# Last unit of a convolution and gated feed-forward kernel: 768 of 1024 tokens projected with Wo standing, the last 256 by tokens

## Chip, cores and metric

The kernel runs on one core of one Trainium2 chip. The metric is the device time in microseconds (us) of one execution, the median of several. All five engines of the core work in it: TensorE (PE, with its weight loads PEld), VectorE (DVE), ScalarE (ACT), GpSimd (POOL) and SyncE (SP, which issues DMAs here).

## What is computed

Two layers follow each other. A causal convolution over 7 positions along the sequence has one softmax-normalised filter for each of 8 heads (24 channels each). Its output, seen as 32768 tokens of 192 channels, goes through a gated feed-forward layer of width 1536. Inputs and output are float32.

```python
def _attn_ref(x, weight):                       # x: 8 x 4096 x 192, weight: 8 x 7
    w = softmax(weight)
    x_pad = concat([zeros(B, 6, D), x], axis=1)
    x_unf = x_pad[:, idx, :].reshape(B, S, K, H, group)
    return einsum('hk,bskhg->bshg', w, x_unf).reshape(B, S, D)

def _moe_ref(x, w_gate, w_val, w_out):          # 192 x 1536, 192 x 1536, 1536 x 192
    gate = maximum(x @ w_gate, 0.0)
    val = x @ w_val
    return gate * val @ w_out
```

## The kernel before, in words

**Tiling.** The eight sequences are taken as two streams (`st` 0 and 1) of four sequences, which are worked on side by side. A window is `WIN` = 512 tokens of each stream, a unit is two windows (`UNIT` = 1024 tokens of each stream), and there are `NUNIT` = 16 units, 0 to 15. All matmuls take 16-bit operands and add up in PSUM in float32. The kernel's order is written out by hand: on each engine the instructions run in the order of the source, and the waits between engines are put in by the framework from what each instruction reads and writes.

**A unit.** `gate_val` (L576 on, matmul at L596) makes the gate and the value of one window in 12 slices `f` of 128 hidden channels. For each slice ScalarE applies the relu to the gate (L607) and VectorE multiplies it by the value out of PSUM into `hT`, 16 bits (L608). `hT` holds hidden channels on its partitions and tokens along them. After both windows the unit is projected by Wo.

**The projection of units 0 to 14** (`project_turn`, L618) holds Wo still and streams tokens. Wo's 192 output channels are cut into three groups `p` of 64 columns, which are two sets of 32 channels. A matmul takes 64 hidden channels by 64 output channels and streams 512 tokens, so that four of them fill the array. The result has output channels on its partitions; VectorE turns it in blocks of 32 by 32 (`turn_out`, L636) into the output tile `o`. `store` (L645) sends `o` to memory with eight DMAs on SP's queue, of 32 partitions each. Rows there are 96 channels, 384 bytes. While this goes on the engines also make the convolution of a later unit (`product`, `lane_rest`, `add`); the last unit has no such work.

**The projection of unit 15** (`project`, L661) goes the other way round: 128 tokens of `hT` are the weights, and Wo's 192 columns stream. It needs no turn, since tokens come out on the partitions. It is called four times, for window 0 and 1 and both streams, 4 x 12 matmuls each. In the fourth call the 512 tokens are cut into pieces of 256, 128 and 128, each with a PSUM tile `ps` of its own. Copies (L672) are ScalarE's but for the second last, which is VectorE's. The stores (L675) go from SP's queue, the very last from ScalarE's.

**Pools.** PSUM has four buffers of `[128, 2, 512]` float32, that is two banks each, handed out in turn. The output pool has two buffers, so the tile `o` of a unit takes the place of that of two units before, and waits until that one's stores are done.

Of the kernel before, what the change touches and what calls it, by code (L numbers as in the profile page):

```python
# [8 lines left out]
FP = mybir.dt.float32  # L9
# [6 lines left out]
def kernel(  # L16
# [12 lines left out]
    nc = tc.nc  # L29

    B, S, D = x.shape
# [4 lines left out]
    NB = B // 2  # L36
    NCH = D // 64
    NBLK = D // 32
    NFF = DFF // 128
    WIN = 512  # L40
# [10 lines left out]
    UNIT = 2 * WIN  # L51
    NUNIT = NB * S // UNIT
# [17 lines left out]
    opool = ctx.enter_context(tc.tile_pool(name="opool", bufs=2))  # L70
    psum = ctx.enter_context(tc.tile_pool(name="psum", bufs=4, space=bass.MemoryType.PSUM))
# [92 lines left out]
    with nc.allow_low_precision("one of the terms is not zero"):  # L164
        nc.vector.tensor_reduce(
            out=Z[:, 112 : 112 + HR],
            in_=eye[:].rearrange("p (g i) -> p i g", i=HR),
# [4 lines left out]
        out=mask[:, :, 0],  # L172
        in_=eye[:].rearrange("p (g i) -> p g i", i=HR),
# [6 lines left out]
    Wo = const.tile([128, NFF, 3, 64], F16)  # L180
# [4 lines left out]
    def none(reps, n):  # L185
        z = zeros[:, 0:1]
        return bass.AP(tensor=z.tensor, offset=z.offset, ap=[z.ap[0], [0, reps], [1, n]])
# [23 lines left out]
    for part, heads in zip(raised, BANDS):  # L211
        nc.tensor.matmul(
            out=part[:, 0 : SUB * len(heads)],
            lhsT=zeros[:],
            rhs=none(len(heads), SUB),
            start=True,
            stop=False,
            skip_group_check=True,
# [65 lines left out]
    for s in (8, 9):  # L284
# [5 lines left out]
        out=mx[:], in_=spread[:, 0, 0:KW], axis=mybir.AxisListType.X, op=ALU.max, negate=True  # L290
# [5 lines left out]
    for jj in STEPS0[:3]:  # L296
# [5 lines left out]
        out=prod[:],  # L302
# [8 lines left out]
    for heads in BANDS:  # L311
        n = len(heads)
        nc.vector.scalar_tensor_tensor(
            out=blocks[:, heads[0] : heads[0] + n, :],
# [12 lines left out]
    for part, heads, to, copy in zip(  # L327
        raised, BANDS, bands, [nc.vector.tensor_copy] * 3
    ):
        n = len(heads)  # L330
        for j in range(128 // HR):
# [3 lines left out]
                out=part[:, 0 : SUB * n].rearrange("p (h t) -> p h t", t=SUB)[:, :, s0 + lo : s0 + hi],  # L335
                lhsT=Z[:, 112 - HR * j : 240 - HR * j],
                rhs=blocks[:, heads[0] : heads[0] + n, lo:hi],
                start=False,
                stop=(j == 128 // HR - 1),
                skip_group_check=True,  # L340
# [5 lines left out]
    for c in range(NCH):  # L346
        r0 = 0
        while r0 < 64:
            h = (64 * c + r0) // G
            r1 = min(64, G * (h + 1) - 64 * c)  # L350
            row = wn[HR * h : HR * h + 8, :]
            for st in range(2):
                nc.sync.dma_start(
                    out=tap[64 * st + r0 : 64 * st + r1, c, :],
                    in_=bass.AP(
                        tensor=row.tensor,
                        offset=row.offset,
                        ap=[row.ap[0], [0, (r1 - r0) // 8], [1, KW]],
                    ),
# [95 lines left out]
    def lane_halo(b):  # L455
        xr = rpool.tile([128, NCH, 2 * (HALO + WIN)], F16, name="x_r")
        if b:
            end = second_start(b - 1) + WIN
            nc.gpsimd.tensor_copy(out=xr[:, :, 0:HALO], in_=xrs[b - 1][:, :, end - HALO : end])
        at = second_start(b)  # L460
        if at > HALO + WIN:
            nc.gpsimd.memset(xr[:, :, at - HALO : at], 0.0)
        xrs[b] = xr

    def lane_turn(b):
        xe, head = xes.pop(b)
        if b not in xrs:
            lane_halo(b)
        xr, at = xrs[b], second_start(b)
        n = 4 * len(windows(b))  # L470
        xp = epool.tile([128, TILES, NCH, 2, 64], F16, name="x_p")
        parts = [slice(0, n)] if head is None else [slice(0, n // 2), slice(n // 2, n)]
        for st in range(2):
            for js in parts:
                nc.gpsimd.tensor_copy(out=xp[:, js, :, st, :], in_=xe[:, js, st, :, :])  # L475
        for j in range(n):
            to = HALO + 128 * j if j < 4 else at + 128 * (j - 4)
            nc.sync.dma_start_transpose(
                out=xr[:, :, to : to + 128],
                in_=xp[:, j].rearrange("p c s r -> p (c s r)"),  # L480
            )
        if head is not None:
            turned = const.tile([HALO, NCH, 2, 64], F16, name="turned")
            for st in range(2):
                nc.gpsimd.tensor_copy(out=turned[:, :, st, :], in_=head[:, st, :, :])
            nc.sync.dma_start_transpose(
                out=xr[:, :, 0:HALO], in_=turned[:].rearrange("p c s r -> p (c s r)")
            )
# [141 lines left out]
    def between_turns(ps):  # L630
        nc.scalar.copy(out=turned_by[:], in_=ps[:, :, 0])  # L631
# [6 lines left out]
            in_=ps[:].rearrange("p b (t c) -> p b t c", c=32),  # L638
        )

    def store(o, bp, w0):
        for q in range(4):
            row0 = (bp + NB * (q // 2)) * S + WIN * w0
            for b in range(2):
                nc.sync.dma_start(  # L645
                    out=out[
                        row0 + WIN * b : row0 + WIN * (b + 1), D // 2 * (q % 2) : D // 2 * (q % 2 + 1)
                    ].rearrange("(t p) d -> p t d", p=32),
                    in_=o[32 * q : 32 * q + 32, :, D // 2 * b : D // 2 * (b + 1)],
                )  # L650

    def project(bp, w, h, st, stores, final, o):


        parts = [range(4)] if not final else [range(2), range(2, 3), range(3, 4)]
        row0 = (bp + NB * st) * S + WIN * w
        for n, qs in enumerate(parts):
            ps = psum.tile([128, 2, 512], FP, name="ps")
            for i, q in enumerate(qs):
                for f in range(NFF):  # L660
                    nc.tensor.matmul(  # L661
                        out=ps[:, i // 2, D * (i % 2) : D * (i % 2) + D],
                        lhsT=h[:, f, st, 128 * q : 128 * (q + 1)],
                        rhs=Wo[:, f, :, :].rearrange("k p (a d) -> k a p d", a=2),
                        start=(f == 0),
                        stop=(f == NFF - 1),
                    )
            os_ = o[:, qs[0] : qs[0] + len(qs), :].rearrange("p (a b) d -> p a (b d)", a=(len(qs) + 1) // 2)
            k = len(qs)
            a, m = (k + 1) // 2, min(k, 2) * D  # L670
            copy = nc.vector.tensor_copy if n == 1 else nc.scalar.copy
            copy(out=os_, in_=ps[:, 0:a, 0:m])  # L672
            nq = max(1, k // stores)
            for q0 in range(qs[0], qs[0] + k, nq):
                (nc.scalar if n == 2 else nc.sync).dma_start(  # L675
                    out=out[row0 + 128 * q0 : row0 + 128 * (q0 + nq), :].rearrange(
                        "(q p) d -> p q d", p=128
                    ),
                    in_=o[:, q0 : q0 + nq, :],
                )  # L680


    dense[0] = xcpool.tile([128, 2, NCH, WIN], F16, name="xc")
# [5 lines left out]
    for c, copy in enumerate((nc.scalar.copy, nc.vector.tensor_copy, nc.scalar.copy)):  # L689
# [7 lines left out]
        out=plain.rearrange("p (c d) -> p c d", d=D), in_=moe_w_out.rearrange("(c p) d -> p c d", p=128)  # L697
    )
    for u in range(NUNIT):
        if u == 0:  # L700
            lane_turn(0)
            wide = plain.rearrange("k (f a p d) -> k f a p d", a=2, p=3, d=32)
            for a in range(2):
                nc.gpsimd.tensor_copy(out=Wo[:, :, :, 32 * a : 32 * a + 32], in_=wide[:, :, a, :, :])
            lane_halo(1)
            lane_load(1)
        hs = [gate_val(u, w) for w in range(2)]
        if u == 0:
            dense[1] = xcpool.tile([128, 2, NCH, WIN], F16, name="xc")
        bp, w0 = u * UNIT // S, u * UNIT % S // WIN  # L710
        lane = None
        if u < NBLOCK:
            lane_first(u)
            lane = lane_rest(u)
        if u == 0:
            conv(2)
        o = opool.tile([128, UNIT // 64, D], FP, name="out_s")
        if u == NUNIT - 1:
            for i in range(4):
                project(bp, w0 + i // 2, hs[i // 2], i % 2, (4, 2, 1, 1)[i], i == 3, o[:, 4 * i : 4 * i + 4, :])  # L720
            continue
        tiles = [None] * 3
        for p, turn in ((0, 0), (1, 0), (0, 1), (2, 0), (1, 1), (2, 1)):
            if turn == 0:
                tiles[p] = psum.tile([128, 2, 512], FP, name="ps")
            project_turn(hs, p, tiles[p], turn)
            if turn == 0:
                between_turns(tiles[p])
                if lane:
                    for k in TAPS[p]:  # L730
                        product(u, k)
                continue
            if lane:
                for _ in range(STEPS[p]):
                    next(lane)
            turn_out(tiles[p], o, p)
        store(o, bp, w0)
        if lane:
            add(u, 0)
        if u + 1 < NBLOCK:  # L740
            lane_turn(u + 1)
        if len(windows(u)) > 1:
            add(u, 1)
        if u + 2 < NBLOCK:
            lane_load(u + 2)
# [30 lines left out]
```

## Time and profile before

Three runs took 761.95 us in the median (761.77 to 762.75). The profiled execution took 761.94 us, with a span of 760.2 us from its first to its last instruction and a granted TensorE clock of 0.999.

| engine | busy us | share of the span | instructions |
|---|---|---|---|
| PE (matmuls) | 756.1 | 99% | 13724 |
| PEld (weight loads) | 471.5 | 62% | 13724 |
| DVE | 675.8 | 89% | 647 |
| ACT | 611.1 | 80% | 681 |
| POOL | 455.3 | 60% | 299 |

How to read it: an engine is busy while one of its instructions runs, and matmuls overlap, so that the mean duration of a matmul (376 ns for 512 columns) is longer than the time by which one follows the other. The chain of waits is followed back from the last instruction, at each step to what released it or to the instruction before it on its engine; 65% of the span is in the gate and value matmuls (L596), 31% in the projection of units 0 to 14 (L618) and 2% in that of unit 15 (L661). Times in the timeline count from the start of the span. SPq and ACTq are the queues from which SP and ScalarE issue DMAs.

### The profile page before, as it was taken

Reading aid. Unit: us, or ns where it says so; the run is one execution under the profiler, and the core shown is the slowest. Engines: PE = TensorE matmul, PEld = TensorE weight load, DVE = VectorE, ACT = ScalarE, POOL = GpSimd, SP = SyncE. Lnnn points to the kernel's source line nnn. Section 1 sums busy time; section 2 is a strip of 40 time slices with the busy share of each in tenths; the row PEclk is TensorE's granted clock in tenths of the full one; section 3 lists DMA queues with packets and bytes.
Section 4 is the critical chain, followed back from the end, with each engine's and each line's share of the span. In section 5 each row is a group of like instructions: output and inputs, shape, how many; then the busy total and the mean of one; then the engine's idle time right before and its main releaser. Section 6 shows DMA issues by size and latency. Waiting matters only on the chain.

```text
span 760.2 us, 30519 instructions
## 1 busy us (share of the span) xinstructions
PE 756.1 (99%) x13724; PEld 471.5 (62%) x13724; DVE 675.8 (89%) x647; ACT 611.1 (80%) x681; POOL 455.3 (60%) x299
## 2 busy tenths in 40 slices
PE   9999999999999999999999999999999999999998
PEld 5555556666666666666666666666666666666668
DVE  7889989998998989989999899998999989897891
ACT  7897887878878788887877878788797887877671
POOL 8519649195591946829377392874919659193600
PEclk9999999999999999999999999999999999999999
DMA  9954532345424444334444334453244532240402
GB/s 149 136 72 92 79 79 52 43 96 75 85 44 51 98 66 85 54 58 83 64 85 73 56 76 54 85 85 64 60 49 93 77 78 52 23 101 7 85 2 85
DMA packets 154146, 54.23 MB, mean 71 GB/s; under 512 B 149264, under 2 KB 154016, under 8 KB 154016
## 3 DMA queue, kind: packets, MB, share of 16 engines
q1 hardware_dynamic: 117488, 37.83, 24.5%
q0 software_dynamic: 36096, 14.16, 16.5%
q8 instruction: 107, 1.75, 0.9%
q10 hardware_dynamic: 432, 0.30, 0.1%
q14 instruction: 23, 0.19, 0.1%
HBM read 29.21 MB, written 25.17 MB: 72 GB/s over the span
## 4 chain that ended last, share of the span: by engine, by line
PE 99%; DMA 1%; ACT 0%; SPq 0%; issue 0%
PE ps L596 65%; PE ps L618 31%; PE ps L661 2%; DMA prod<-in_x_dram 1%; PE ps L390 0%; PE ps L413 0%; ACT out_s L122 0%; SPq L112 0%; ACT out_s L672 0%
## 5 line engine op out<-in xcount | busy, mean ns | idle before, releaser
L608 DVE TENSOR_TENSOR hT<-gr,ps 128x1024 f16<-128x1024 f16 (+1 forms) x385 | 468.9, 1218 | 35.4 <-ACT gr L607 8.3
L607 ACT ACTIVATE gr<-ps 128x1024 f16<-128x1024 f32 (+1 forms) x385 | 393.2, 1022 | 114.2 <-PE ps L596 114.2
L525 POOL TENSOR_TENSOR prod<-prod,prod 128x896 f32<-128x896 f32 x145 | 302.8, 2088 | 253.0 <-DVE prod L559 243.8
L596 PE MATMUL ps<-xc,Wv 64*64 64x512 f16 (+1 forms) x4464 | 320.6, 376 | 0.0
L596 PE MATMUL ps<-xc,Wg 64*64 64x512 f16 (+1 forms) x4464 | 320.6, 376 | 0.0
L618 PE MATMUL ps<-hT,Wo 64*64 64x512 f16 x4320 | 235.9, 376 | 0.0
L596 PEld LDWEIGHTS <-Wg 64*64 64x64 f16 (+1 forms) x4464 | 152.6, 107 | 96.0
L596 PEld LDWEIGHTS <-Wv 64*64 64x64 f16 (+1 forms) x4464 | 152.5, 106 | 96.0 <-DVE hT L608 0.3
L618 PEld LDWEIGHTS <-Wo 64*64 64x64 f16 x4320 | 144.2, 107 | 88.8 <-issue 0.2
L513 ACT ACTIVATE prod<-x_r,tap 128x1024 f32<-128x1024 f16 (+2 forms) x195 | 182.8, 1017 | 0.0
L549 DVE SCALAR_TENSOR_TENSOR acc<-x_r,tap,acc 128x1024 f32<-128x1024 f16 (+3 forms) x150 | 118.0, 852 | 0.0
L636 DVE STREAM_TRANSPOSE out_s<-ps 128x1024 f32<-128x1024 f32 x45 | 56.1, 1247 | 28.4 <-PE ps L618 24.4
L525 POOL TENSOR_TENSOR xc<-prod,prod 128x896 f16<-128x896 f32 x29 | 60.6, 2088 | 2.3
L475 POOL COPY x_p<-x_e 128x1536 f16<-128x1536 f16 (+1 forms) x32 | 42.2, 1352 | 0.6 <-DMA x_e<-in_x_dram 0.6
L254 POOL DMA_DIRECT2D x_e<-in_x_dram x30 | 26.5, 888 | 0.0
L549 DVE SCALAR_TENSOR_TENSOR xc<-x_r,tap,acc 128x1024 f16<-128x1024 f16 (+3 forms) x30 | 25.1, 837 | 0.0
L538 ACT ACTIVATE acc<-x_r,tap 128x1024 f32<-128x1024 f16 (+3 forms) x30 | 22.5, 801 | 0.1
L631 ACT COPY turned_by<-ps 128x2 f32<-128x2 f32 x45 | 7.0, 155 | 16.5 <-PE ps L618 14.5
L661 PEld LDWEIGHTS <-hT 128*128 128x128 f16 x192 | 15.8, 98 | 0.4 <-issue 0.4
L661 PE MATMUL ps<-Wo,hT 128*128 128x192 f16 x192 | 16.0, 246 | 0.0
L672 ACT COPY out_s<-ps 128x768 f32<-128x768 f32 (+2 forms) x5 | 3.2, 639 | 12.7 <-PE ps L661 12.7
L672 DVE COPY out_s<-ps 128x192 f32<-128x192 f32 x1 | 0.4, 357 | 13.3 <-PE ps L661 13.3
(58 smaller groups left out, 68.7 us busy)
## 6 DMA issues: line engine op xcount, KB each, us to landing
out_dram<-out_s SPq DMA_DIRECT2D x123, 192.0 KB
x_e<-in_x_dram POOLq DMA_DIRECT2D x28, 384.0 KB, 6.3
x_r<-x_p SPq DMA_TRANSPOSE x116
prod<-in_moe_w_out_dram POOLq DMA_DIRECT2D x1, 576.0 KB, 9.3
out_s<-in_x_dram POOLq DMA_DIRECT2D x2, 240.0 KB, 6.0
out_dram<-out_s SPq DMA_DIRECT2D x5, 96.0 KB
prod<-in_x_dram SPq DMA_DIRECT2D x2, 192.0 KB
out_s<-in_x_dram POOLq DMA_DIRECT2D x2, 192.0 KB, 7.1
```

What stands on the lines that cost most here:

```text
L254: nc.gpsimd.dma_start(out=xe[:, 0:n, st, :, :].rearrange("p j c r -> p j (c r)"), in_=bass.AP(tensor=x.tensor, offset=x.offset + row * D, ...
L475: nc.gpsimd.tensor_copy(out=xp[:, js, :, st, :], in_=xe[:, js, st, :, :])
L513: nc.scalar.activation(out=both(prods[b, k], b, at, n), in_=shifted(b, c, k, t, n), func=ACTF.Copy, scale=tap[:, c, k : k + 1],)
L525: nc.gpsimd.tensor_tensor(out=acc if k < KW - 1 else xcs[b][:, w, :, :].rearrange("p c t -> p (c t)")[:, LDVE : NCH * WIN], in0=acc, in1=p ...
L538: nc.scalar.activation(out=both(accs[b], b, at, n), in_=shifted(b, c, 0, t, n), func=ACTF.Copy, scale=tap[:, c, 0:1],)
L549: nc.vector.scalar_tensor_tensor(out=result(b, at, n) if k == KW - 1 else both(acc, b, at, n), in0=shifted(b, c, k, t, n), scalar=tap[:, c ...
L596: nc.tensor.matmul(out=pss[i][q : q + M, st, :], lhsT=W[64 * st : 64 * st + 64, c, 128 * f + q : 128 * f + q + M], rhs=xcb[64 * st : 64 * ...
L607: nc.scalar.activation(out=gr[:, sts], in_=pss[0][:, sts], func=ACTF.Relu)
L608: nc.vector.tensor_tensor(out=h[:, f, sts], in0=gr[:, sts], in1=pss[1][:, sts], op=ALU.mult)
L618: nc.tensor.matmul(out=ps[64 * st : 64 * st + 64, b, :], lhsT=Wo[64 * r : 64 * r + 64, f, p, :], rhs=hs[b][64 * r : 64 * r + 64, f, st, :] ...
L636: nc.vector.transpose(out=o[:].rearrange("p t (b d) -> p b t d", b=2)[:, :, :, 32 * p : 32 * p + 32], in_=ps[:].rearrange("p b (t c) -> p ...
L661: nc.tensor.matmul(out=ps[:, i // 2, D * (i % 2) : D * (i % 2) + D], lhsT=h[:, f, st, 128 * q : 128 * (q + 1)], rhs=Wo[:, f, :, :].rearran ...
```

## The change

Only the last unit's projection and the stores of units are touched. `project` goes, `last_project` comes:

- Window 0 (all 512 tokens of both streams) and the first 256 tokens of window 1 are projected with Wo as the weights, and turned by VectorE. Unlike units 0 to 14, a matmul takes all 128 hidden channels of a slice and 64 output channels, so that two of them (one for each stream, in the lower and the upper half of the columns) fill the array. There are 3 x 12 x 2 of them over 512 tokens and as many over 256. `tiles[0]` to `tiles[2]` hold window 0 in bank 0 and window 1 in bank 1, and are turned one by one, three turns for each window; the results are stored as in the other units, by four DMAs for each window.
- The last 256 tokens of each stream are projected by tokens as before, in three pieces: 256 tokens of stream 0 (in `tiles[3]`, bank 0), then 128 and 128 of stream 1 (in `tiles[3]`, bank 1, and in `tiles[0]`, bank 0). They are copied by ScalarE, VectorE and ScalarE into `rest`, a second output tile, and stored from SP's queue twice and from ScalarE's.
- `store` can cut its first `halved` DMAs into two. Unit 14 does so with six of its eight, and issues 14.

TensorE has the same number of matmuls in the last unit's projection, 192, in both kernels: 144 turned ones and 48 by tokens after.

```diff
+    def store_part(o, bp, w, b, q, t0, t1):
+        row0 = (bp + NB * (q // 2)) * S + WIN * w
+        nc.sync.dma_start(
+            out=out[
+                row0 + 32 * t0 : row0 + 32 * t1, D // 2 * (q % 2) : D // 2 * (q % 2 + 1)
+            ].rearrange("(t p) d -> p t d", p=32),
+            in_=o[32 * q : 32 * q + 32, t0:t1, D // 2 * b : D // 2 * (b + 1)],
+        )
+
+    def store(o, bp, w0, halved=0):
+        for n in range(8):
+            q, b = n // 2, n % 2
+            cuts = [0, WIN // 64, WIN // 32] if n < halved else [0, WIN // 32]
+            for t0, t1 in zip(cuts, cuts[1:]):
+                store_part(o, bp, w0 + b, b, q, t0, t1)
+
+    def last_project(bp, w0, hs, o):
+        END = 256
+        rest = opool.tile([128, UNIT // 64, D], FP, name="out_s")
+        tiles = [psum.tile([128, 2, 512], FP, name="ps") for _ in range(4)]
+        for b in range(2):
+            n = WIN - END * b
+            nt = n // 32
+            for p in range(3):
+                for f in range(NFF):
+                    for st in range(2):
+                        nc.tensor.matmul(
+                            out=tiles[p][64 * st : 64 * st + 64, b, 0:n],
+                            lhsT=Wo[:, f, p, :],
+                            rhs=hs[b][:, f, st, 0:n],
+                            start=(f == 0),
+                            stop=(f == NFF - 1),
+                            tile_position=(0, 64 * st),
+                            skip_group_check=True,
+                        )
+                nc.vector.transpose(
+                    out=o[:].rearrange("p t (b d) -> p b t d", b=2)[:, b, 0:nt, 32 * p : 32 * p + 32],
+                    in_=tiles[p][:, b, 0:n].rearrange("p (t c) -> p t c", c=32),
+                )
+            for q in range(4):
+                store_part(o, bp, w0 + b, b, q, 0, nt)
+        pieces = [
+            (tiles[3][:, 0, :], 0, range(2), nc.scalar, nc.sync),
+            (tiles[3][:, 1, :], 1, range(1), nc.vector, nc.sync),
+            (tiles[0][:, 0, :], 1, range(1, 2), nc.scalar, nc.scalar),
+        ]
+        for ps, st, qs, engine, queue in pieces:
             for i, q in enumerate(qs):
+                t0 = WIN - END + 128 * q
                 for f in range(NFF):
                     nc.tensor.matmul(
-                        out=ps[:, i // 2, D * (i % 2) : D * (i % 2) + D],
-                        lhsT=h[:, f, st, 128 * q : 128 * (q + 1)],
+                        out=ps[:, D * i : D * i + D],
+                        lhsT=hs[1][:, f, st, t0 : t0 + 128],
                         rhs=Wo[:, f, :, :].rearrange("k p (a d) -> k a p d", a=2),
...
+            o2 = rest[:, 2 * st + qs[0] : 2 * st + qs[0] + k, :]
+            (engine.copy if engine is nc.scalar else engine.tensor_copy)(
+                out=o2.rearrange("p q d -> p (q d)"), in_=ps[:, 0 : D * k]
+            )
...
         if u == NUNIT - 1:
-            for i in range(4):
-                project(bp, w0 + i // 2, hs[i // 2], i % 2, (4, 2, 1, 1)[i], i == 3, o[:, 4 * i : 4 * i + 4, :])
+            last_project(bp, w0, hs, o)
             continue
...
-        store(o, bp, w0)
+        store(o, bp, w0, 6 if u == NUNIT - 2 else 0)
```

More of the change, by code (lines that the diff above doesn't have):

```diff
@@ L639, in turn_out @@
         )
[L641 to L649, printed above, removed]
-                )
[L652 to L658, printed above, removed]
+    def store_part(o, bp, w, b, q, t0, t1):
[6 more added lines that the diff above has]
+        )
@@ L667, in project @@
                     )
-            os_ = o[:, qs[0] : qs[0] + len(qs), :].rearrange("p (a b) d -> p a (b d)", a=(len(qs) + 1) // 2)
             k = len(qs)
[L670 to L680, printed above, removed]
+            o2 = rest[:, 2 * st + qs[0] : 2 * st + qs[0] + k, :]
+            (engine.copy if engine is nc.scalar else engine.tensor_copy)(
+                out=o2.rearrange("p q d -> p (q d)"), in_=ps[:, 0 : D * k]
+            )
+            row0 = (bp + NB * st) * S + WIN * (w0 + 2) - END + 128 * qs[0]
+            queue.dma_start(
+                out=out[row0 : row0 + 128 * k, :].rearrange("(q p) d -> p q d", p=128), in_=o2
+            )
     dense[0] = xcpool.tile([128, 2, NCH, WIN], F16, name="xc")
```

## The prediction

> **What bounds the kernel now.** I read the chain of waits first, because it says which engine the end follows. Its last pieces, in order of time (start us, length us, what):
>
> ```profile
> 694.69 15.54 PE ps L618 x288
> 710.23 31.08 PE ps L596 x576
> 741.31 15.96 PE ps L661 x192
> 757.27 0.02 issue
> 757.30 0.32 ACT out_s L672
> ```
>
> TensorE's stages follow each other without a gap, and after the last projection stand only one ScalarE copy and its store. So only TensorE time in the last unit, or work after the last matmul, can move the end. Two rates come from here: a 64x64 projection runs 288 matmuls in 15.54 us, four at a time, so 215.8 ns for a group of four over 512 columns; the gate and value stage gives 31.08/576, or 53.96 ns for one matmul.
>
> Next the last unit in order of time (start, length, engine, line, tile, count, idle time before and its releaser):
>
> ```profile
> 740.48 0.84 PE L596 MATMUL ps<-xc,Wv 64*64 64x512 f16 x12
> ...
> 741.25 16.01 PE L661 MATMUL ps<-Wo,hT 128*128 128x192 f16 x192
> ...
> 755.32 0.48 ACT L672 COPY out_s<-ps 128x384 f32<-128x384 f32 x1 [1.18 <-PE ps L661]
> 755.82 0.37 SPq L675 DMA_DIRECT2D out_dram<-out_s  x1
> 756.69 0.34 SPq L675 DMA_DIRECT2D out_dram<-out_s  x1
> 756.77 0.49 PE L661 MATMUL ps<-Wo,hT 128*128 128x192 f16 x4
> ...
> 757.30 0.32 ACT L672 COPY out_s<-ps 128x192 f32<-128x192 f32 x1 [1.50 <-PE ps L661]
> 757.65 0.37 ACTq L675 DMA_DIRECT2D out_dram<-out_s  x1
> ```
>
> The first of the 192 matmuls starts at 741.25 and the 189th at 756.77, so one starts every 15.52/188 = 82.55 ns and the stream is through at 741.25 + 192 x 82.55 ns = 757.10. The last copy starts 0.20 us later: that is what a result needs from the end of its stream to an engine that waits for it. From there to the end of the span (760.2) go 2.9 us of copy, store and landing.
>
> The projection loses nothing to waits: 192 rows of 192 columns at 82.55 ns use the whole array, as the 64x64 form does. Scaled to the work of the last unit (the same 288 x 64x64x512), the other form takes 15.54 us against 15.85, so no rearrangement that keeps the full array busy at these rates gains more than about 0.3 us.
>
> **The change part by part.** Everything before 741.25 on TensorE stays. What follows replaces the 15.85 us.
>
> *Turned part, window 0.* 72 matmuls with 128 rows and 64 columns of weights in two column halves, 512 tokens each: 36 pairs. The trace has no 128x64 tile. Two of them fill the array as four 64x64 do, so I take 215.8 ns a pair: 7.77 us. That two column halves with all rows run side by side is shown by the narrower column tiles of the convolution:
>
> ```profile
> 20.26 0.83 PE L596 MATMUL ps<-xc,Wv 64*128 64x512 f16 x6
> 21.02 1.59 PE L390 MATMUL ps<-band,out_s 118*32 118x112 f16 x120
> 22.53 0.82 PE L596 MATMUL ps<-xc,Wg 64*128 64x512 f16 x6
> ```
>
> 120 of them, four across, start within 1.51 us: 12.6 ns each, weight load included.
>
> *Turned part, window 1.* 36 pairs over 256 tokens. Half of 215.8 is 107.9 ns; L661's rate by column (82.55/192) gives 110.1. I take 109: 3.92 us. Here each pair has two weight loads to hide in 109 ns. Bounds: 25 ns for 64 columns (two 32-column loads at 12.6), wholly hidden, and the 82.55 ns in which L661 passes a full 128x128 load, twice, 165 ns a pair and 5.94 us, 2.0 more. A 64-column load at 54 ns each in L618 (four in 215.8) is nearest in shape and just fits, so I keep 3.92.
>
> *The load rule.* The profile's groups (busy us, mean ns; idle us) say of the loads:
>
> ```profile
> L661 PE MATMUL ps<-Wo,hT 128*128 128x192 f16 x192 | 16.0, 246 | 0.0
> L661 PEld LDWEIGHTS <-hT 128*128 128x128 f16 x192 | 15.8, 98 | 0.4 <-issue 0.4
> ```
>
> A load of 98 ns into all rows passes under a stream that advances every 82.55 ns, so it overlaps. The Trainium skill, "TensorE: Matmul & The Clock Gate", Part 3 (packing small matmuls), says that a weight load overlaps with running matmuls only when the row group differs. By that rule this change would suffer, since both column halves use all rows; L661 speaks against it. It is a rival below.
>
> *A change of tile form.* The group of 12 that starts at 740.48 is through at 741.13 (12 x 53.96 ns) and L661 starts at 741.25: 0.12 us. L596 before the convolution, 6 x 107.9 from 20.26, ends at 20.91, and L390 starts at 21.02: 0.11. Before there is one such change, after there are two (64x64 to 128x64, then to 128x128): +0.12 us.
>
> *Last 256 tokens of each stream.* 48 of L661's matmuls, the same shape: 48 x 82.55 = 3.96 us.
>
> *A wait that was not there.* The three pieces before had a PSUM tile each. Now the first (256 tokens, stream 0) and the second (128 tokens, stream 1) share `tiles[3]`, in its two halves. In the built program the second piece's first matmul waits for the count that ScalarE's copy of the first piece raises. TensorE has nothing else queued to do: behind that matmul stand the other 23, the two last copies and the last two stores. From stream end to copy start 0.20 us, the copy itself 0.48 (128x384 row above), then TensorE's waking. The nearest row for that (three casts, so 0.41 us each):
>
> ```profile
> 5.15 1.22 DVE L342 CAST band<-ps 128x336 f16<-128x336 f32 x3 [0.27 <-PE ps L334]
> ...
> 5.71 0.48 PE L390 MATMUL ps<-band,out_s 118*32 118x112 f16 x24 [0.17 <-DVE band L342]
> ```
>
> The first cast ends at 5.56, the matmul starts at 5.71: 0.15. A store follows its copy by 0.02 (755.32 + 0.48 to 755.82). Between these I take 0.10. The stall is 0.20 + 0.48 + 0.10 = 0.78 us, from 0.70 to 0.83.
>
> *The other waits of TensorE* are covered. Window 1's group p waits for VectorE's turn of window 0 in the same tile. That takes 0.20 us, then half of a full turn:
>
> ```profile
> L636 DVE STREAM_TRANSPOSE out_s<-ps 128x1024 f32<-128x1024 f32 x3 | 3.7, 1250 | 5.7 <-PE ps L618 5.7
> ```
>
> So 0.83 us, while two other groups run, at least 2 x 1.31 us; uncovered it would cost up to 0.83 each. The third piece reuses `tiles[0]`, turned some 7 us earlier.
>
> *VectorE, ScalarE, GpSimd.* VectorE gains six turns (3 x 0.63, 3 x 0.31); it idles 13.3 us here in the trace. ScalarE loses three copies of 0.80 us, off the path. The tail keeps its form: 384, 192 and 192 columns copied, the last stored from ScalarE's queue. GpSimd has nothing here.
>
> *Stores.* Eight turned stores, 1.18 MB in all, now precede the pieces in SP's queue. What such a store costs is seen in unit 14's eight, 1.57 MB (issues, then stretches with DMA share and GB/s last):
>
> ```profile
> 711.63 6.83 SPq L645 DMA_DIRECT2D out_dram<-out_s  x8
> ...
> 712.20:712.80 0.60, 0.60 (x16) 0.41 (x12) 0.60 (x1) 0.58 (x1) 0.60 (x1) 1.00 0.45 90
> 712.80:720.40 7.60, 7.60 (x147) 4.73 (x140) 7.16 (x7) 5.97 (x7) 7.37 (x4) 1.00 0.92 185
> ```
>
> Data moves some 0.85 us after the issue, at 185 GB/s with nearly all engines busy. The four of window 0 are issued at 741.25 + 7.77 + 0.20 + 0.63 = 749.85, window 1's by about 753.6, so 1.18 MB run from 750.7 to 757.1. The first two pieces, 0.29 MB at 197 to 239 GB/s, are through by 758.6 at most:
>
> ```profile
> 755.00:757.00 2.00, 2.00 (x27) 2.00 (x25) 0.36 (x1) 0.48 (x1) 0.00 (x0) 1.00 0.74 239
> 757.50:758.00 0.50, 0.00 (x0) 0.00 (x0) 0.00 (x0) 0.12 (x1) 0.00 (x0) 1.00 0.62 197
> 758.00:758.50 0.50, 0.00 (x0) 0.00 (x0) 0.00 (x0) 0.00 (x0) 0.00 (x0) 1.00 0.00 0
> 758.50:759.00 0.50, 0.00 (x0) 0.00 (x0) 0.00 (x0) 0.00 (x0) 0.00 (x0) 1.00 0.62 197
> ```
>
> The last store, issued 0.7 us later than now, moves from about 759.2. It stays clear by some 0.6 us. Unit 14's stores become 14 instead of 8; SP then idles long (longest wait first to last: total us, times, longest):
>
> ```profile
> SPq L675 <- ACT out_s L672: 33.9, 4, 27.7
> ```
>
> Six more issues of under 0.9 us each fit in 27.7 us, so that edit costs nothing; without this idle time it would cost up to 5 us.
>
> *Sum.* 7.77 + 3.92 + 0.12 + 3.96 + 0.78 = 16.55 us in place of 15.85: +0.70. The profiled execution took 761.94 us (span 760.2), 0.01 below the median 761.95, so the forecast is 761.94 + 0.70 = 762.6. From the unknowns: -0.10 (waking, window 1 at 107.9) to +0.2 (0.15 waking, 110.1, a tile change of 0.2).
>
> **The rivals.** (a) The wait costs nothing, so the work alone decides: 0.70 - 0.78 = -0.08, 761.9. For it: both forms are near the array's rate. Against it: nothing else is in TensorE's queue to cover a copy of 0.48.
>
> (b) Slower: the turned matmuls can't hide their loads. If loads and streams alternate in all 144, each adds between 25 and 54 ns: 3.6 to 7.8 us, taken at 54, the row with the same column count, 770.4. This is what the rule above would make of it. If they are only short of room in window 1, the price is the 2.0 worked out there: 764.6. It begins to decide when a load needs over 54 ns. L390's 12.6 ns and L661's overlap speak against both.
>
> (c) Slower: the stores become the end. In the first 2 us of unit 14's stores the queue moved less:
>
> ```profile
> 712.00:714.00 2.00, 2.00 (x44) 1.27 (x40) 1.93 (x2) 1.51 (x2) 1.97 (x1) 1.00 0.71 142
> ```
>
> At 142 GB/s throughout, the turned stores last until 759.0, the pieces to 760.4, and the last store's 0.1 MB to about 760.8 instead of 759.7: 1.1 more, 763.7. It decides once the backlog passes 759.2. Against it: that stretch holds the 0.5 us before the first byte.
>
> (d) Faster: 128x64 pairs run leaner than 64x64 groups. 15.85 us can't shrink by more than some tenths, and the stall must go too; 761.6 at best.
>
> **How the numbers follow.** 0.2% of this time is 1.5 us, about what a measurement of this kernel can tell from no change: 760.4 to 763.5 is "within". Forecast 0.77 (own range 762.3 to 762.9 from the unknowns), (a) 0.07, (d) 0.02, (b) 0.09 in both sizes, (c) 0.05. Within: 0.77, 0.07 and 0.02, less 0.03 for a measurement that strays: 0.83. Slower: 0.09 + 0.05 and 0.01 of the straying, 0.15. Faster: the other 0.02. The range goes from 0.1 below (a), 761.8, to (c), 763.7, and leaves out (b), (d) and little else.
>
> **What would show it.** Right: a single gap in TensorE's time, about 0.8 us, between the piece of 256 tokens and the next, released by ScalarE's copy; the turned groups in about 7.8 and 3.9 us; the last copy near 758.0. Wrong: no gap there; window 1's groups well over 1.31 us each; loads in the chain; DMA traffic without a pause up to the last store; a last store that lands more than 2.6 us after its issue.

## The result: 1.1 us more, 0.66 us of it in TensorE and the rest behind the last store

The changed kernel takes 763.21 us in the median of 22 runs (762.71 to 763.84), the kernel before 762.11 (761.77 to 762.75, 22 runs). The ratio is 1.0013 with a 95% interval of 1.0007 to 1.0019: slower by 1.10 us, within the 0.2% that were named as no change. The forecast was 762.6, range 761.8 to 763.7, with a rise of 0.70.

The profiled execution took 762.83 us with a span of 761.1 (761.94 and 760.2 before). The end of its chain of waits (start us, length us, what):

```profile
710.03 31.08 PE ps L596 x576
741.11 11.82 PE ps L670 x144
752.93 2.10 PE ps L694 x24
755.03 0.02 issue
755.05 0.49 ACT out_s L703
755.54 0.04 issue
755.58 2.15 PE ps L694 x24
757.73 0.02 issue
757.76 0.32 ACT out_s L703
```

TensorE's last projection, one piece before, is now three pieces with a ScalarE copy between them. The same stretch in the timeline (start, length, engine, line, tile, count, idle time before and its releaser):

```profile
741.04 11.89 PE L670 MATMUL ps<-hT,Wo 128*64 128x512 f16 x144
743.86 0.72 DVE L679 STREAM_TRANSPOSE out_s<-ps 128x512 f32<-128x512 f32 x1 [1.08 <-PE ps L670]
746.45 0.72 DVE L679 STREAM_TRANSPOSE out_s<-ps 128x512 f32<-128x512 f32 x1 [1.87 <-PE ps L670]
749.04 0.72 DVE L679 STREAM_TRANSPOSE out_s<-ps 128x512 f32<-128x512 f32 x1 [1.88 <-PE ps L670]
...
750.35 0.45 DVE L679 STREAM_TRANSPOSE out_s<-ps 128x256 f32<-128x256 f32 x1 [0.59 <-PE ps L670]
751.66 0.45 DVE L679 STREAM_TRANSPOSE out_s<-ps 128x256 f32<-128x256 f32 x1 [0.86 <-PE ps L670]
...
752.86 2.15 PE L694 MATMUL ps<-Wo,hT 128*128 128x192 f16 x24
752.97 0.45 DVE L679 STREAM_TRANSPOSE out_s<-ps 128x256 f32<-128x256 f32 x1 [0.86 <-PE ps L670]
755.05 0.48 ACT L703 COPY out_s<-ps 128x384 f32<-128x384 f32 x1 [13.52 <-PE ps L694]
755.58 2.14 PE L694 MATMUL ps<-Wo,hT 128*128 128x192 f16 x24 [0.57 <-ACT out_s L703]
...
758.11 0.37 ACTq L707 DMA_DIRECT2D out_dram<-out_s  x1
```

The 24 matmuls from 752.86 are streamed by 754.84 (24 x 82.55 ns). The next one starts at 755.58, so TensorE stands still for 0.74 us: 0.21 to the copy's start, 0.48 copy, 0.05 waking. The idle time of 0.57 that the row names is shorter, because it counts from the modelled end of the last matmul.

Executions start differently: the last projection begins at 741.31 before and 741.11 after, which is the scatter of the first loads. I therefore count from that start. To the issue of the last store it is 758.11 - 741.11 = 17.00 us, before 757.65 - 741.31 = 16.34: +0.66. From there to the end of the span it is 3.02 us, before 2.58. So 0.66 us of the loss is in TensorE, where 0.70 were forecast, and 0.44 lies behind the last store's issue, where nothing was expected. Of those 0.44 the profile shows only SP's instructions at the very end. Before (count, shortest/median/longest ns, first and last start):

```profile
L771 SPq EVENT_SEMAPHORE  x11: 17/28/28, 757.1 to 760.2; - x11
...
L771 SPq DRAIN  x3: 7/7/13, 759.4 to 759.7; - x3
```

and after:

```profile
L799 SPq EVENT_SEMAPHORE  x11: 17/28/28, 757.6 to 761.1; - x11
...
L799 SPq DRAIN  x3: 7/7/136, 760.1 to 760.6; - x3
```

Before, SP's first drain comes 1.75 us after the last store's issue (757.65), after it comes 2.0 us after it (758.11), and one drain takes 136 ns instead of at most 13.

### The profile page after: what moved, and what is told of

It reads as the page before. It is cut to its first block, busy times and chain, and to the rows that moved or that the text cites. A ratio compares the mean times of both kernels' runs of the same rounds, so it can differ in the third digit from the quotient of the medians.

```text
span 761.1 us, 30537 instructions
## 1 busy us (share of the span) xinstructions
PE 756.0 (99%) x13724; PEld 455.0 (60%) x13724; DVE 679.4 (89%) x653; ACT 608.4 (80%) x678; POOL 455.1 (60%) x299
## 3 DMA queue, kind: packets, MB, share of 16 engines
q8 instruction: 107, 1.75, 0.9%
## 4 chain that ended last, share of the span: by engine, by line
PE 99%; DMA 1%; ACT 0%; SPq 0%; issue 0%
PE ps L596 65%; PE ps L618 31%; PE ps L670 2%; PE ps L694 1%; DMA prod<-in_x_dram 1%; PE ps L390 0%; PE ps L413 0%; ACT out_s L122 0%; SPq L112 0%; ACT out_s L703 0%
## 5 line engine op out<-in xcount | busy, mean ns | idle before, releaser
L596 PEld LDWEIGHTS <-Wv 64*64 64x64 f16 (+1 forms) x4464 | 150.3, 106 | 98.1 <-DVE hT L608 0.3
L596 PEld LDWEIGHTS <-Wg 64*64 64x64 f16 (+1 forms) x4464 | 147.5, 107 | 101.3
L618 PEld LDWEIGHTS <-Wo 64*64 64x64 f16 x4320 | 139.2, 107 | 93.8 <-issue 0.2
L670 PE MATMUL ps<-hT,Wo 128*64 128x512 f16 (+1 forms) x144 | 11.9, 326 | 0.0
L670 PEld LDWEIGHTS <-Wo 128*64 128x64 f16 x144 | 7.9, 110 | 4.1 <-issue 0.4
L679 DVE STREAM_TRANSPOSE out_s<-ps 128x512 f32<-128x512 f32 (+1 forms) x6 | 3.5, 584 | 7.1 <-PE ps L670 7.1
```

Of the source, the lines that this page charges most:

```text
L596: nc.tensor.matmul(out=pss[i][q : q + M, st, :], lhsT=W[64 * st : 64 * st + 64, c, 128 * f + q : 128 * f + q + M], rhs=xcb[64 * st : 64 * ...
L618: nc.tensor.matmul(out=ps[64 * st : 64 * st + 64, b, :], lhsT=Wo[64 * r : 64 * r + 64, f, p, :], rhs=hs[b][64 * r : 64 * r + 64, f, st, :] ...
L670: nc.tensor.matmul(out=tiles[p][64 * st : 64 * st + 64, b, 0:n], lhsT=Wo[:, f, p, :], rhs=hs[b][:, f, st, 0:n], start=(f == 0), stop=(f == ...
```

## The experiments

All the kernels compute the whole of the reference's output. Each was profiled once; all but one were timed in five rounds (6 to 11 executions) beside 27 to 32 of the kernel before, whose median was 762.13 to 762.23 us on those occasions. The recorded 95% interval of such a ratio reaches some 0.0009 to either side, or 0.7 us. Smaller differences of the medians are therefore no proof by themselves, and the argument goes by the profiles, where the same stretch can be compared from kernel to kernel.

### Is it the wait, and does it cost what the gap shows?

`own_tile_p` gives the second piece a tile that was turned long before. One turned store goes to GpSimd's queue, for a reason that the third run shows.

```diff
-            (tiles[3][:, 1, :], 1, range(1), nc.vector, nc.sync),
+            (tiles[1][:, 0, :], 1, range(1), nc.vector, nc.sync),
...
-                store_part(o, bp, w0 + b, b, q, 0, nt)
+                store_part(o, bp, w0 + b, b, q, 0, nt, nc.gpsimd if b == q == 0 else None)
```

> The second piece gets tiles[1] (bank 0), turned long before, so that it no longer waits for ScalarE's copy; window 0's first turned store goes from GpSimd's queue. Theory (the wait costs 0.74 us): the gap in TensorE between the pieces goes, the last copy comes 16.0 us after the last unit's projection starts (16.72 in the changed kernel), time 762.5. Rival (the stores set the end, the gap is only a wait within their time): gap gone, time still 763.2.

`after_p` has the second of these edits alone.

> The changed kernel with window 0's first turned store from GpSimd's queue and nothing else: the control of the run above. Theory: 763.2 like the changed kernel, gap of 0.74 us kept. Rival (a store on GpSimd's queue has a price of its own at the end): above 763.4.

Measured: `own_tile_p` 762.49 us (762.19 to 763.67), `after_p` 763.08 (762.74 to 763.62). The medians differ by 0.59 us. In the profile of `own_tile_p` the 48 matmuls of the pieces run without a gap:

```profile
741.43 11.82 PE ps L670 x144
753.25 4.08 PE ps L694 x48
757.33 0.02 issue
757.35 0.32 ACT out_s L703
```

From the start of the projection to the last copy it is 15.92 us, in `after_p` 757.97 - 741.32 = 16.65: 0.73 less. The wait is real, and nothing covers it. But the median of `own_tile_p` is still 0.36 above that of the kernel before, although its TensorE part is 0.07 shorter than before.

`own_tile` has the first edit alone.

> Only the tile of the second piece is changed, no store is moved. In this program the second piece's store also waits until the last store, ScalarE's, has landed, since both take the same of eight completion counters in turn. Theory (gap gone, but two stores now follow each other): the second piece's store is issued about 1.9 us after the last store's issue, and the end comes 1.9 us later than in own_tile_p, 764.4. Rival (a store's place in the queue is free, only TensorE's end counts): 762.5.

Measured: 764.13 us (763.91 to 765.18), 1.6 above `own_tile_p` where 1.9 were expected; without the gap, and slower than the changed kernel. In its timeline the two stores from SP's queue stretch over 3.70 us, and its waits (what waited, for what; us, times, longest) name a DMA:

```profile
755.95 3.70 SPq L707 DMA_DIRECT2D out_dram<-out_s  x2
...
757.55 0.37 ACTq L707 DMA_DIRECT2D out_dram<-out_s  x1
```

```profile
SPq L707 <- DMA out_dram<-out_s: 2.9, 1, 2.9
```

The framework gives DMAs eight completion counters in turn, in the order in which it meets them while building. Here ScalarE's last store and the second piece's store, eight DMAs apart, share a counter, and the second piece's store waits until the last one has landed. So removing the gap only paid where the counters were looked at too.

### A second wait

`two_waits` puts the third piece into the second's bank:

```diff
-            (tiles[0][:, 0, :], 1, range(1, 2), nc.scalar, nc.scalar),
+            (tiles[3][:, 1, 192:512], 1, range(1, 2), nc.scalar, nc.scalar),
```

> The changed kernel, with the third piece in the same half of the same tile as the second, so that its first matmul waits for VectorE's copy of the second. Theory (a wait with nothing queued behind it costs the drain, the copy and the waking): a second gap of 0.20 + 0.36 + 0.05 = 0.61 us, time 763.8. Rival (TensorE's gaps are covered by the stores): 763.2.

Measured: 764.14 us (763.48 to 764.54). The timeline has two gaps:

```profile
755.94 1.15 PE L694 MATMUL ps<-Wo,hT 128*128 128x192 f16 x12 [0.57 <-ACT out_s L703]
757.59 1.15 PE L694 MATMUL ps<-Wo,hT 128*128 128x192 f16 x12 [0.50 <-DVE out_s L703]
```

Twelve matmuls are streamed in 0.99 us, by 756.93, so the second gap is 0.66 us, 0.05 more than expected. In time it cost 0.93 over the changed kernel's 763.21, measured on another occasion; from the projection's start to the end of the span it is 0.64.

### What costs behind the last store?

The suspicion fell on the longer list of stores. `before_halved` is the kernel before with six of unit 14's stores cut in two, `before_halved_u0` the same with six of unit 0's, `not_halved` the changed kernel with whole stores.

```diff
-        store(o, bp, w0)
+        store(o, bp, w0, 6 if u == NUNIT - 2 else 0)      # before_halved; u == 0 in before_halved_u0
```

> The kernel before, with six of unit 14's eight stores cut in two. Theory: no change, 762.1 (762.0 to 762.3), the stores drain long before the last unit's projection. Rival (the longer list of DMAs has a price at the end of the kernel, such as one more fetch of instructions, and explains part of what the changed kernel lost behind its last copy): 762.4 or more, with an instruction transfer in the last microsecond.

> The kernel before, with six stores cut in two in unit 0 instead of unit 14: the same number of SP instructions as in before_halved, but 650 us before the end. Theory (length of SP's program): 762.6 to 762.8 as before_halved, last store's issue to end 3.0 us or more. Rival (the cut stores of unit 14 themselves delay something in the last unit): 762.1 as before.

> The changed kernel with unit 14's stores whole (8 instead of 14 DMAs). Theory (SP's longer program costs at the end of the kernel): the gap of 0.74 us stays, the time from the last store's issue to the end of the span goes back from 3.0 to 2.55 us, 762.7. Rival (that time differs by chance from execution to execution): 763.2 as in the changed kernel.

Measured: `before_halved` 762.76 us (762.18 to 763.49), `before_halved_u0` 762.70 (762.36 to 763.44), both 0.5 to 0.6 above before; so the edit that I had costed at nothing costs half a microsecond, wherever it stands. (The intervals of both ratios still reach down to 0.9997 and 0.9998; the table below has the same 0.58 us from the profiles.) The sign that the rival of `before_halved` named was there as well, a transfer of instructions in the last microsecond. It is shown below. But `not_halved` took 763.11 (762.96 to 764.92), only 0.1 below the changed kernel. My theory of the program's length alone falls, since it promised 762.7.

`own_tile_p_nh`, that is `own_tile_p` with whole stores, missed as well:

> The second piece in a tile of its own, window 0's first turned store on GpSimd's queue, and unit 14's stores whole. Theory (wait and program length are all that the change costs): 762.1, as before, within 0.2. Rival (the turned stores near the end cost too): 762.4 or more.

Measured: 762.77 us (762.32 to 763.78), no better than `own_tile_p`. That is the rival's number; whether the turned stores are the reason is tested by `own_tile_short` below, which keeps them.

SP's trace records show where the time goes. Below is when SP's instructions start, in us after the issue of ScalarE's last store: the first check of a completion counter that starts after the store has landed, how many checks follow it, the first two drains, and the end of the span. The counter that the last store holds and the number of SP's instructions are those of the built programs.

```
kernel             counter  SP instr.  landed  checks after  drain 1  drain 2  end
before                7       336      1.670        0         1.735    1.800   2.578
changed kernel        7       342      1.681        0         2.040    2.237   3.016
before_halved         5       342      1.672        2         2.181    2.377   3.157
before_halved_u0      5       342      1.682        2         2.200    2.392   3.171
own_tile_p            6       341      1.678        1         1.843    2.188   3.083
not_halved            1       336      1.695        6         2.127    2.197   2.976
own_tile_p_nh         0       335      1.666        7         2.165    2.235   3.006
```

In all of them SP sees the last store landed 1.67 to 1.70 us after its issue. Two things differ. SP checks the eight counters in a fixed order, 0 to 7, one after the other, some 0.06 us each: a last store on counter 7 leaves no check behind it, one on counter 0 leaves seven (0.43 us from 1.735 to 2.165). And SP pauses some 0.3 us longer before one of its drains where its program has 341 or 342 instructions. With 342 it is the first drain, with 341 the second, one instruction later in the list: the pause sits at a fixed place of the program. Programs of 333 to 337 instructions show none.

The traces say more about that place. They hold two records fewer than SP has instructions. In all eight profiles of programs with 341 or 342 instructions the pause stands before SP's 336th record, and the other six profiles end with the 335th or earlier. Two more such places are in all fourteen profiles: before SP's 80th record it pauses 0.44 to 0.46 us and before its 208th 0.34 to 0.35 us, where the records around them follow by 0.04 to 0.06, although cut or moved stores put other instructions there. The three places are 128 records apart. And 0.63 to 0.65 us after the start of the 336th record a transfer of 8192 bytes of the kind `instruction` starts, in all eight; in the other six the next such transfer starts 0.95 us or more after the end of the span. Here are the transfers from the last store's issue to the end of the span (queue, kind: packets, MB, share of 16 engines), in the kernel before:

```profile
q10 hardware_dynamic: 144, 0.10, 12.0%
q1 hardware_dynamic: 128, 0.09, 10.5%
```

and in `before_halved`, where the last line's one packet starts 0.33 us before the end:

```profile
q10 hardware_dynamic: 144, 0.10, 9.9%
q1 hardware_dynamic: 120, 0.08, 8.1%
q14 instruction: 1, 0.01, 0.9%
```

The changed kernel has both: its six extra stores put the last store on counter 7 (with whole stores it would be counter 1), and lengthen SP's program past the place of the pause. What they save they give back.

Three kernels test this, each with a store or two of unit 0 moved to GpSimd's queue (whose counters are others) or one of unit 14's cut, to set counter and length.

```diff
+        if u == 0:                                        # after_short: two; own_tile_short: one
+            for k in range(6, 8):
+                store_part(o, bp, w0 + k % 2, k % 2, k // 2, 0, WIN // 32, nc.gpsimd)
...
-        store(o, bp, w0)
+        store(o, bp, w0, 1 if u == NUNIT - 2 else 0)      # before_cut1, in the kernel before
```

> The changed kernel with unit 14's stores whole and two of unit 0's stores on GpSimd's queue, behind its sums. So ScalarE's last store takes completion counter 7, the last that SP waits for at the end, as before, and SP's program has 333 instructions (336 before, 342 in the changed kernel). Theory (behind the last store the end costs by the counter's place, some 0.06 us for each counter still to be checked, and 0.4 us for a fetch of SP's last instructions): last store's issue to end of span 2.58 us as before, gap of 0.74 us kept, time 762.8. Rival (that stretch varies by chance or by the turned stores): 3.0 us, 763.2.

> The same with the second piece in a tile of its own (tiles[1]), one of unit 0's stores and window 0's first turned store on GpSimd's queue; last store on counter 7, 334 SP instructions. Theory: no gap, 2.58 us behind the last store's issue, from the start of the last projection to the end of the span 18.85 us (18.91 before, 20.0 in the changed kernel), time 762.1, the same as before within 0.2. Rival (something else of the turned part costs): 762.5 or more.

> The kernel before with one of unit 14's stores cut in two: SP has one instruction more (337), and ScalarE's last store takes counter 0, so that SP has seven checks left when it lands. Theory: 0.4 us more between the last store's issue and the end (2.98 us), 762.55; if 337 instructions already need the extra fetch, 3.4 us and 763.0. Rival: 2.58 us, 762.15.

Measured, with the same records:

```
kernel             counter  SP instr.  landed  checks after  drain 1  drain 2  end
after_short           7       333      1.676        0         1.741    1.805   2.581
own_tile_short        7       334      1.669        0         1.734    1.803   2.574
before_cut1           0       337      1.670        7         2.169    2.234   3.004
```

All three ends came as expected within 0.03 us, and so did the 18.85 us of `own_tile_short` (18.84). Its turned stores cost nothing more, so they are not the reason for the time of `own_tile_p_nh`. In time `own_tile_short` took 762.00 us (761.73 to 763.38), the ratio to before 1.0000 with an interval of 0.9991 to 1.0009, and `before_cut1` 762.69 (762.39 to 762.88), 0.56 over the kernel before where 0.43 were expected. `after_short` took 763.02 (762.48 to 764.09), 0.2 more than expected, though its profile has the short end; the interval is wider than that. The chain of `own_tile_short`:

```profile
741.39 11.82 PE ps L668 x144
753.21 4.08 PE ps L692 x48
757.29 0.02 issue
757.31 0.32 ACT out_s L701
```

Counted from the start of the last projection to the issue of ScalarE's last store, and from there to the end of the span, the two parts together give each kernel's time against the kernel before:

```
kernel             to last store's issue  to the end   sum   against before   median against before
before                    16.34             2.58      18.92
changed kernel            17.00             3.02      20.02       +1.10             +1.10
after_p                   17.00             3.00      20.00       +1.08             +0.95
after_short               17.00             2.58      19.58       +0.66             +0.89
not_halved                17.01             2.98      19.99       +1.07             +0.88
two_waits                 17.66             3.00      20.66       +1.74             +1.91
own_tile_p                16.27             3.08      19.35       +0.43             +0.36
own_tile_p_nh             16.28             3.01      19.29       +0.37             +0.54
own_tile_short            16.27             2.57      18.84       -0.08             -0.13
own_tile                  16.27             4.80      21.07       +2.15             +2.00
before_halved             16.34             3.16      19.50       +0.58             +0.63
before_halved_u0          16.33             3.17      19.50       +0.58             +0.47
before_cut1               16.33             3.00      19.33       +0.41             +0.56
```

The sums come from one execution each, the medians from 6 to 22; they agree within 0.25 us. What supports the smaller differences is that the stretch behind the last store repeats: 2.57 to 2.58 us in the three kernels on counter 7 without the pause, 3.16 and 3.17 in the two on counter 5 with it, 3.00 and 3.01 in the two on counter 0 without it. No version beats the kernel before by more than its measurement can tell: `own_tile_short`, without the gap and without the pause and on counter 7, is 0.08 us shorter in its profile.

### Do the weight loads of column halves hide?

`split_mix` has no gap and streams window 1's three groups in parts of 128, 64 and 32 tokens, with weight loads for each part. It ran once, for its profile (770.26 us).

```diff
-                for f in range(NFF):
+                PART = (128, 64, 32)[p] if b else n
+                for f, at in [(f, at) for at in range(0, n, PART) for f in range(NFF)]:
...
-                            rhs=hs[b][:, f, st, 0:n],
+                            rhs=hs[b][:, f, st, at : at + PART],
```

> The second piece in a tile of its own, and window 1's three turned groups streamed in parts of 128, 64 and 32 tokens instead of 256, each part with its own weight loads. Theory (loads of 64 columns in one column half pass under the other streams, at 12.6 ns a load and matmul or a little more): the three groups take 1.34, 1.4 and 2.4 us. Rival (a load needs 54 ns, or does not overlap since both halves use all rows): 2.6, 5.2 and 10.4 us. The second piece's store also waits for the last store here, so its end is not read.

The turns in its timeline mark the ends of the groups:

```profile
749.71 0.72 DVE L680 STREAM_TRANSPOSE out_s<-ps 128x512 f32<-128x512 f32 x1 [1.87 <-PE ps L671]
...
751.05 0.45 DVE L680 STREAM_TRANSPOSE out_s<-ps 128x256 f32<-128x256 f32 x1 [0.62 <-PE ps L671]
752.57 0.45 DVE L680 STREAM_TRANSPOSE out_s<-ps 128x256 f32<-128x256 f32 x1 [1.07 <-PE ps L671]
...
753.93 2.20 PE L671 MATMUL ps<-hT,Wo 128*64 128x32 f16 x128 [0.75 <-issue]
758.22 0.82 PE L671 MATMUL ps<-hT,Wo 128*64 128x32 f16 x23 [2.09 <-issue]
758.98 6.18 PE L695 MATMUL ps<-Wo,hT 128*128 128x192 f16 x48
759.09 0.45 DVE L680 STREAM_TRANSPOSE out_s<-ps 128x256 f32<-128x256 f32 x1 [6.07 <-PE ps L671]
```

Parts of 128 tokens take 751.05 - 749.71 = 1.34 us for 24 pairs (56 ns a pair, where a quarter of 215.8, the streams alone, would be 54), parts of 64 take 1.52 for 48 pairs, 32 ns with two weight loads in it. So the loads of 64 columns into all rows hide beside running streams; one comes through every 16 ns, or takes at most 32 if the two halves load side by side, and the rival with 54 ns, 5.2 us for this group, is out. The Trainium skill, "TensorE: Matmul & The Clock Gate", Part 3, lets loads overlap only where the row group differs; both halves use all rows here, and the trace disagrees. Parts of 32 tokens missed the expected 2.4 us. At best 64 pairs took 2.20 us, 34 ns each, no faster than with 64 tokens. And their group ran into something else: TensorE stood still for 0.75 and 2.09 us without a wait that the profile names, so that the group took 6.52 us from turn to turn. That is told at the end.

## Why the prediction was right, and its step that failed

**The turned groups.** 11.82 us in the chain from 741.11 to 752.93; the terms were 7.77 + 3.92 + 0.12 = 11.81. The rate of 64x64 groups carries over to 128x64 pairs, with 512 tokens and with 256: the turns shown above start 2.59 us apart in window 0, or 215.8 ns for each of 12 pairs, and 1.31 us apart in window 1, or 109 ns. Rival (b) is out, in both sizes.

**The wait.** Forecast 0.78, measured 0.74: the copy starts after 0.21, lasts 0.48, and waking took 0.05 instead of 0.10. Rival (a) is out: the gap is there, and taking it away gave 0.59 us in the medians and 0.73 in the profile.

**The other waits** are covered as said, though the turns were slower than half of a full one: 0.72 and 0.45 us for 512 and 256 columns, where 0.63 and 0.31 stood. TensorE did not wait for one of them.

**The stores.** The last transfer was to start clear of the turned ones. In the changed kernel's stretches (DMA share and GB/s last):

```profile
750.50:757.00 6.50, 5.93 (x88) 5.59 (x83) 1.38 (x4) 0.48 (x1) 0.00 (x0) 1.00 0.93 201
...
757.50:758.00 0.50, 0.22 (x3) 0.00 (x0) 0.00 (x0) 0.24 (x1) 0.00 (x0) 1.00 0.00 0
758.00:758.50 0.50, 0.00 (x0) 0.00 (x0) 0.00 (x0) 0.07 (x1) 0.00 (x0) 1.00 0.62 197
758.50:759.00 0.50, 0.00 (x0) 0.00 (x0) 0.00 (x0) 0.00 (x0) 0.00 (x0) 1.00 0.03 9
759.00:759.50 0.50, 0.00 (x0) 0.00 (x0) 0.00 (x0) 0.00 (x0) 0.00 (x0) 1.00 0.59 188
```

The backlog ends by 757.5, the second piece's store passes after 758.0, and the last has the engines to itself from 759.0. Rival (c) is out. Its price had been worked out wrongly: at 142 GB/s throughout, the 0.29 MB of the first two pieces would last from 759.0 to 761.0 and the last store's 0.1 MB to 761.7, which is 2.0 us more than 759.7 and not 1.1.

**The step that failed** is "that edit costs nothing", said of unit 14's 14 stores. I looked at their traffic and at SP's idle time, which do hide them, but not at what they do to the end of the kernel. Two terms were missing: the pause before SP's 336th record, which with the longer drain behind it puts SP's second drain 0.44 us later after the last store in the changed kernel than in the kernel before, and the counter's place, which stays at 7 only because of these cuts. The forecast of 0.70 for the whole was therefore 0.4 too low. The measured 763.21 lies above the 762.3 to 762.9 that its unknowns gave (the forecast also started from 761.94, 0.17 below the later median); it is inside the stated range because rival (c), which did not happen, had set the upper end at 763.7. So the mechanism in TensorE was right by reasoning, and the place in the range is in part luck. "The tail keeps its form" was right for copies, stores and landing (1.68 us against 1.67), and wrong for what SP does after it. One of the prediction's own signs of being wrong, a last store that lands more than 2.6 us after its issue, counted that whole stretch as landing; it came (3.02 us), but not through the store.

What SP waits for in the pause is not shown. That it turns there from one block of 128 instructions to the next fits the three places, 128 records apart, and the transfer of 8192 bytes (64 for each of 128) behind the last of them; but that transfer starts after the pause, not in it, so this stays an inference.

## What to carry to other kernels

Before sharing a PSUM tile between pieces in the tail, ask what TensorE has queued behind the wait: with nothing there, the wait costs the drain, the copy and the waking, 0.74 us here, and another tile whose last reader is long done costs nothing. In the last microseconds, count the instructions and completion counters of the engine that closes the kernel: cutting early stores in two moved the end by 0.4 to 0.6 us in the profiles without touching any work near it. And count from the start of the last stage when differences are below the scatter of the first loads: the last projection started between 741.11 and 742.29 us in these profiles.

## What had not been expected of the hardware

In `split_mix` TensorE stood still for 2.09 us, from 756.13 to 758.22, without a wait that the profile names, and the granted clock fell (engines' busy time, then clock, DMA share and GB/s):

```profile
753.93:756.13 2.20, 2.20 (x128) 2.10 (x128) 0.00 (x0) 0.00 (x0) 0.00 (x0) 1.00 0.80 153
756.13:756.43 0.30, 0.00 (x1) 0.00 (x0) 0.00 (x0) 0.00 (x0) 0.00 (x0) 0.99 0.00 0
756.43:758.22 1.79, 0.00 (x0) 0.00 (x0) 0.00 (x0) 0.00 (x0) 0.00 (x0) 0.50 0.00 0
758.22:763.25 5.03, 5.03 (x50) 4.76 (x51) 0.45 (x1) 0.21 (x1) 0.00 (x0) 0.50 0.36 80
763.25:765.20 1.95, 1.92 (x23) 1.68 (x21) 0.36 (x1) 0.27 (x1) 0.00 (x0) 1.00 0.34 105
```

The 48 matmuls by tokens behind it took 6.13 us in the chain instead of the 4.08 of `own_tile_p`. By this record the clock was halved at 756.43, only 0.30 us into the pause, so the 2.09 us cannot be what halved it. In the 3.4 us before, TensorE had stood still for 1.05 us (0.75 and these 0.30) and run matmuls of 32 columns for the rest. The Trainium skill, "TensorE: Matmul & The Clock Gate", Part 1, gives about 3.4 us as the window of idleness after which the clock is halved; here far less idleness was enough. In `two_waits` gaps of 0.74 and 0.66 us, 1.40 us within 2.4 us, left the clock at 1.00, so gaps alone do not decide it either. What does is not shown.

The two pauses lie 256 of TensorE's records apart, 128 loads and 128 matmuls, which ran in 2.20 us. Transfers of instructions, 16 KB each on a queue of their own, start at 751.29, 755.75 and 759.36 us there. That TensorE ran out of instructions would fit, and is not shown.
